# Another order of the attention's parts on all engines, and the strided probabilities normalised on GpSimd

## The chip, the core and the metric

The kernel runs on one core of a Trainium2 chip. The metric is the device time of one execution, in microseconds (us). The core has five engines that run at the same time, each through its own list of instructions in order: TensorE (PE; PEld is its weight load), VectorE (DVE), ScalarE (ACT), GpSimd (POOL) and SyncE (SP), which here only issues the DMA transfers. The transfers of SyncE's queue are carried by 16 DMA engines. Semaphores make an engine wait for another one.

## What is computed

Three stages follow each other: masked attention over 4 batches of 8 heads (576 positions, 64 channels), a soft mixture of 8 experts with 4 slots each, and a two-layer network with a squared ReLU. Half of the heads see a local window of 32 positions, the other half every 32nd position.

```python
scores = scale * np.matmul(q, k.transpose(0, 1, 3, 2))
mask_local = (rel >= 0) & (rel < stride)                       # heads 0 to 3
mask_strided = (rel >= 0) & (pos[None, :] % stride == pos[:, None] % stride)   # heads 4 to 7
attn = softmax(where(mask, scores, -1e9)); x = attn @ v        # x as (2304, 512)

logits = x @ phi
d = softmax(logits, over tokens); slot_input = d.T @ x         # 32 slots of 512
slot_out[e] = relu(slot_input[e] @ w1[e]) @ w2[e]              # 8 experts
y = softmax(logits, over slots) @ slot_out
out = relu(y @ w_in) ** 2 @ w_out
```

The expert weights are 33.5 MB in 64 pieces of 512 KB (`w1_slot`, `w2_slot`, issued at L120), q, k and v together some 14 MB. `w_in` and `w_out` come as 64-bit numbers and are narrowed on chip.

## The kernel before

Attention works on 16 units, each two heads of one batch. Even units are local, odd ones strided. A unit passes through these parts: `ld` (q and k loads; L379 and L390 for local, L385 and L390 for strided units; the L390 loads are small), `lv` (values: L399 local, L403 strided), `Tq` and `Tk` (transposes of q and k on TensorE, L501 and L503 or L506), `q` (ScalarE scales the transposed q out of PSUM, L525) and `k` (two copies on ScalarE, L488), `S` (scores, L550 to L574), `s` (maximum and subtraction on VectorE, L588 and L589 or L595 and L599), `e` (exponential on ScalarE, L610), `n` (strided units alone: sum, reciprocal and multiply, L617 to L620), `PT` (transposes of the probabilities, L629 or L634), `p` (their eviction: ScalarE for local units; for strided ones L648 on ScalarE and L650 on VectorE), `A` (times the values, L665 or L673), `a` (eviction, with the division for local units, L685 to L687), `X` and `x` (transposes of the output, L709 or L706, and eviction). For local units GpSimd copies the values once more, shifted by a block (`vs`, L410, two copies). After each four units `L` forms the logits (L728, L734), and `R1` to `R3` (L746 to L811) update the running softmax over tokens.

Two lists of words, `PIPE`, set the order. The program walks through the units u; at an even u it goes through the first list, at an odd u through the second, and `A-1` means part A of unit u-1. Each engine executes its own share of these parts in the order of the words (a pin ties each instruction of a computing engine behind the one before it). The DMA queue isn't pinned: a scheduler sorts its transfers when the program is built, and SyncE then issues them strictly in that order, so a transfer that waits for a buffer holds up those behind it. `ft` fetches weights: 1 or 2 pieces per unit in the first half of attention, 4 per pair in the second (`PACE`), into a ring of 27 buffers; buffers of attention are added to them as its last units finish. `cv` narrows one piece of `w_in` (L218 on ScalarE, L223 to L227 on VectorE). `F1` is a filler matmul on the mask (L153) that keeps TensorE at work; `DRAIN` sets more of them ahead of the last units' parts, and `KEEP` those in the end part of attention (`st_end`, L824).

All parts share PSUM as four pairs of banks. `pair` hands them out in turn, skipping the held ones; a part that gets a pair waits until its last user has been evicted. Which user that is follows from the order of the words.

After attention the experts' layers run pair by pair (L1030, L1060), freeing weight buffers as they go, and from about 183 us the last network (L1190, L1229) until the end.

The change touches `KEEP`, `DRAIN`, `PIPE` and `ON_ACT`. `ON_ACT` says for some evictions whether ScalarE does them: `pS` for the two halves of `p` of strided units, `n` for the engine of the multiply in `n` (0: VectorE; 2: GpSimd, but for the last unit).

## Time and profile before

| | |
|---|---|
| time, median of 3 runs (lowest to highest) | 418.67 us (415.93 to 420.39) |
| profiled execution | 419.13 us; the trace spans 417.2 us of it |
| busy in the span: PE, PEld, DVE, ACT, POOL | 387.8, 303.0, 238.5, 233.7, 86.7 us |
| chain that ended last | PE 64%, DMA 20%, DVE 5%, POOL 5% |
| mean granted TensorE clock | 0.979 of full speed |
| attention, expert layers, last network | to 147.6, to about 183, to 417 us |

The busy times say little on their own, since the stages have different limits. The rows further down are read by place: which stretch, what its engines do there, and who waits for whom. "PEclk" in them is the granted clock of TensorE as a share of 2.4 GHz, the DMA share the mean busy share of the 16 DMA engines (it goes over 1 where packets overlap).

### The profile page before, as it was taken

The numbers are of one execution on the slowest core, as the hardware profiler recorded it, in microseconds if no ns is written. First come the engines' busy times: TensorE is split into PE (matmuls) and PEld (weight loads), VectorE is DVE, ScalarE is ACT, GpSimd is POOL, SyncE is SP. The second block draws the span as 40 slices with busy tenths as digits, with TensorE's granted clock in tenths as the row PEclk, the third lists the DMA queues.
The fourth block names the chain that finished last, engine by engine and source line by source line (L and its number), as shares of the span: only waits on it lengthen the run. The fifth ranks groups of instructions, "written<-read, shape, count | busy, mean of one in ns | idle before, by whom it ended". The sixth has DMA issues, their size and how long they took to land.

```text
span 417.2 us, 9176 instructions
## 1 busy us (share of the span) xinstructions
PE 387.8 (93%) x3652; PEld 303.0 (73%) x3653; DVE 238.5 (57%) x452; ACT 233.7 (56%) x475; POOL 86.7 (21%) x121
## 2 busy tenths in 40 slices
PE   6898698989788899999999999999999999999996
PEld 3777486778666645467788887888887888878884
DVE  6456447766365461138856564867657766745434
ACT  3365536655543430039778686666666676666760
POOL 6302211102112020035610252111424103420000
PEclk9899779999899999999999999999999999999999
DMA  6897988998999999996212131221000000004033
GB/s 154 224 278 238 192 219 247 269 305 222 247 375 270 391 361 418 418 418 280 86 66 101 51 102 57 95 101 50 2 0 0 2 1 2 0 1 152 36 117 151
DMA packets 52202, 69.87 MB, mean 167 GB/s; under 512 B 31744, under 2 KB 37120, under 8 KB 52160
## 3 DMA queue, kind: packets, MB, share of 16 engines
q1 hardware_dynamic: 52160, 69.29, 51.9%
q8 instruction: 29, 0.48, 0.5%
q14 instruction: 13, 0.11, 0.1%
HBM read 64.55 MB, written 4.72 MB: 166 GB/s over the span
## 4 chain that ended last, share of the span: by engine, by line
PE 64%; DMA 20%; DVE 5%; POOL 5%; ACT 2%; issue 2%; SPq 2%; POOLq 0%; DVEq 0%; ACTq 0%
PE banks L1229 43%; DMA space<-in_v_dram 10%; DMA w<-in_moe_w_dram 7%; PE banks L1190 4%; DMA space<-in_k_dram 3%; PE banks L1030 2%; POOL space L410 2%; PE banks L665 2%; PE banks L1120 2%; PE banks L501 1%; POOL w L1105 1%; PE banks L554 1%; POOL w L1104 1%; PE banks L709 1%; PE banks L728 1%
## 5 line engine op out<-in xcount | busy, mean ns | idle before, releaser
L1229 PE MATMUL banks<-w 128*128 128x512 f32 x864 | 218.5, 395 | 1.6 <-POOL w L1105 1.2
L1229 PEld LDWEIGHTS banks<-w 128*128 128x128 f32 x864 | 159.5, 188 | 37.1 <-POOL w L1105 2.9
L1206 DVE TENSOR_TENSOR w<-r,w 128x384 fp32r<-128x384 f32 (+1 forms) x97 | 57.4, 594 | 73.0 <-ACT w L1205 72.9
L1197 ACT ACTIVATE r<-banks 128x384 f32<-128x384 f32 (+1 forms) x96 | 47.0, 490 | 53.1 <-PE banks L1190 46.2
L1203 ACT ACTIVATE r<-r 128x384 f32<-128x384 f32 (+1 forms) x96 | 50.3, 524 | 3.0
L1205 ACT CAST w<-r 128x384 fp32r<-128x384 f32 (+1 forms) x97 | 49.5, 510 | 4.1 <-DVE r L1202 0.6
L488 ACT COPY space<-banks 64x576 f32<-64x576 f32 (+2 forms) x64 | 34.7, 542 | 12.9 <-PE banks L153 10.3
L410 POOL COPY space<-space 32x1088 f32<-32x1088 f32 x16 | 17.7, 1107 | 103.0 <-DMA space<-in_v_dram 75.1
L220 POOL TENSOR_SCALAR nm<-w 128x512 f32<-128x512 f32 x28 | 24.0, 859 | 63.0 <-DMA w<-in_moe_w_out_dram 32.3
L1244 DVE TENSOR_TENSOR part<-banks,part 128x512 f32<-128x512 f32 (+1 forms) x55 | 34.9, 673 | 2.4 <-PE banks L1229 2.3
L1190 PE MATMUL banks<-cT,A 128*128 128x384 f32 x96 | 32.0, 335 | 0.0
L1104 POOL CAST w<-wf 128x512 fp32r<-128x512 f32 x16 | 11.8, 741 | 94.8 <-PE banks L1229 37.2
L501 PE MATMUL banks<-ident,space 128*128 128x128 f32 x128 | 22.8, 305 | 4.1 <-DVE space L589 2.4
L224 DVE SCALAR_TENSOR_TENSOR nm<-w,nm 128x512 uint32<-128x512 uint32 x32 | 22.3, 696 | 1.1
L501 PEld LDWEIGHTS banks<-ident,space 128*128 128x128 f32 x128 | 15.9, 161 | 8.1 <-DVE space L589 3.1
L1105 POOL TENSOR_TENSOR w<-wf,w 128x512 fp32r<-128x512 f32 x16 | 21.5, 1341 | 1.4
L223 DVE TENSOR_SCALAR nm<-nm 128x512 uint32<-128x512 uint32 x32 | 14.6, 457 | 12.3 <-POOL nm L220 9.2
L665 PE MATMUL banks<-space 128*32 128x130 f32 x288 | 13.7, 295 | 7.9 <-POOL space L410 4.8
L1190 PEld LDWEIGHTS banks<-cT,A 128*128 128x128 f32 x96 | 18.0, 188 | 3.9 <-ACT r L1197 0.2
L610 ACT ACTIVATE space<-space 128x640 f32<-128x640 f32 (+1 forms) x16 | 9.4, 590 | 17.4 <-DVE space L589 14.4
L488 DVE COPY space<-banks 128x576 f32<-128x576 f32 (+1 forms) x16 | 9.7, 607 | 15.9 <-ACT space L488 12.8
L665 PEld LDWEIGHTS banks<-space 128*32 128x32 f32 x288 | 9.7, 117 | 10.5 <-POOL space L410 6.4
(186 smaller groups left out, 446.2 us busy)
## 6 DMA issues: line engine op xcount, KB each, us to landing
w<-in_moe_w_dram SPq DMA_DIRECT2D x48, 512.0 KB
w<-in_moe_w_in_dram SPq DMA_DIRECT2D x16, 512.0 KB
space<-in_moe_w_dram SPq DMA_DIRECT2D x16, 512.0 KB
w<-in_moe_w_out_dram SPq DMA_DIRECT2D x16, 512.0 KB
space<-in_v_dram SPq DMA_DIRECT2D x32, 144.0 KB
out_dram<-part SPq DMA_DIRECT2D x17, 256.0 KB
space<-in_k_dram SPq DMA_DIRECT2D x16, 128.0 KB
space<-in_q_dram SPq DMA_DIRECT2D x16, 128.0 KB
```

Of the source, the lines that this page charges most:

```text
L410: nc.gpsimd.tensor_copy(vL[64 * h:64 * h + 32, 1:18, h, 0:D], vL[64 * h + 32:64 * h + 64, 0:17, h, 0:D])
L488: return (nc.scalar.copy if act else nc.vector.tensor_copy)(out=out, in_=in_)
L501: nc.tensor.transpose(out=pf[:, w * t:w * t + 128], in_=m[:, ts(t, 128)], identity=ident)
L665: nc.tensor.matmul(out=pv[c, n // 4] if n < 18 else pv[c, 4].rearrange("p (h e) -> p h e", h=2), lhsT=w, rhs=i, start=True, stop=True, til ...
L1105: nc.gpsimd.tensor_tensor(out=lo, in0=r, in1=hi.bitcast(F32), op=ALU.subtract)
L1190: nc.tensor.matmul(out=ps[:, 0:HB], lhsT=A4[c][:, ts(f % QF, 128)], rhs=cT4[:, c0:c0 + HB], start=True, stop=True)
L1197: nc.scalar.activation(out=r[:, cuts[0]], in_=ps[:, cuts[0]], func=AF.Relu)
L1203: nc.scalar.activation(out=r[:, cuts[0]], in_=r[:, cuts[0]], func=AF.Square)
L1205: nc.scalar.copy(out=gh[:, x], in_=r[:, x])
L1206: nc.vector.tensor_tensor(out=gl[:, x], in0=r[:, x], in1=gh[:, x].bitcast(F32), op=ALU.subtract)
L1229: nc.tensor.matmul(out=acc[t], lhsT=a[:, ts(t, 128)], rhs=wo[f][:, ts(w, 512)], start=(first and k == 0), stop=(last and k == 2),)
L1244: nc.vector.tensor_tensor(out=pt[:, cs], in0=acc[t][:, cs], in1=pt[:, cs], op=ALU.add)
```

## The change

The two lists of `PIPE` are rewritten; the strided multiply of `n` goes to GpSimd in seven of eight units; both halves of the strided `p` are done by VectorE; a few filler counts change. The table itself:

```diff
-KEEP = (4, 0, 0, 5, 0)
-DRAIN = dict(S0=0, PT1=0, A1=3, X1=4, PT0=4, A0=0)
+KEEP = (4, 0, 0, 8, 0)
+DRAIN = dict(S0=0, PT1=0, A1=3, X1=4, PT0=1, A0=1)
 PIPE = (
-    "PT-1 p-1 S+0 vs+0 x-3 ft Tq+1 s+0 R2 Tk+1 R3 X-2 e+0 cv q+1 ld+3 L-2 A-1 k+1 ld+4 R1 F1 F1 x-2 n+0 F1 F1 a-1".split(),
-    "lv+0 PT-1 cv p-1 S+0 s+0 Tq+1 q+1 e+0 Tk+1 A-1 n+0 k+1 lv+1 ft vs+0 L-2 X-2 a-1 R2 R1 R3".split(),
+    "PT-1 p-1 lv+0 S+0 x-3 Tk+1 ft s+0 Tq+1 L-2 R2 vs+0 R3 ld+3 q+1 X-2 e+0 R1 n+0 cv F1 ld+4 A-1 lv+1 x-2 k+1 F1 F1 F1 a-1".split(),
+    "PT-1 p-1 S+0 s+0 cv Tq+1 ft e+0 n+0 Tk+1 A-1 L-2 a-1 R2 k+1 vs+0 R1 X-2 q+1 R3".split(),
 )
-ON_ACT = dict(kL=(1, 1), kS=(1, 1), pL=1, pS=(1, 0), xL=0, xS=1, aS=(1, 1, 1, 0), q=1, n=0)
+ON_ACT = dict(kL=(1, 1), kS=(1, 1), pL=1, pS=(0, 0), xL=0, xS=1, aS=(1, 1, 1, 0), q=1, n=2)
```

Three places show what that does to the engines' lists. The first is the DMA queue in the pair of units 8 and 9: the local q and k of unit 12 (L379, L390), the strided values of unit 9 (L403) and weights (L120). Before:

```order
L379 DMA space<-in_q_dram 128x4x64 x2
L379 DMA space<-in_k_dram 128x4x64 x2
L390 DMA space<-in_k_dram 64x2x64
L390 DMA space<-in_q_dram 64x2x64
L403 DMA space<-in_v_dram 36x1024 x2
L120 DMA w<-in_moe_w_dram 128x1024 x4
```

The same place in the changed program:

```order
L379 DMA space<-in_k_dram 128x4x64 x2
L379 DMA space<-in_q_dram 128x4x64
L390 DMA space<-in_k_dram 64x2x64
L379 DMA space<-in_q_dram 128x4x64
L390 DMA space<-in_q_dram 64x2x64
L120 DMA w<-in_moe_w_dram 128x1024
L403 DMA space<-in_v_dram 36x1024 x2
L120 DMA w<-in_moe_w_dram 128x1024 x3
```

The keys now come before the queries, one small load moves ahead of the last large one, and one weight piece moves ahead of the strided values.

The second place is VectorE in the odd unit 7, where a piece of `w_in` is narrowed (L223 to L227). Before:

```order
L223 TENSOR_SCALAR nm<-nm 128x512
L224 SCALAR_TENSOR_TENSOR nm<-w,nm 128x512
L227 SCALAR_TENSOR_TENSOR wi<-w,nm 128x512
L595 TENSOR_REDUCE mx<-banks 128x2x4x2
L599 TENSOR_TENSOR space<-banks,mx 128x8x36
L617 TENSOR_REDUCE sm<-space 128x16
L618 TENSOR_SCALAR sm<-sm 128x16
L619 RECIPROCAL sm<-sm 128x16
L620 TENSOR_TENSOR space<-space,sm 128x8x36
```

The same place in the changed program:

```order
L595 TENSOR_REDUCE mx<-banks 128x2x4x2
L599 TENSOR_TENSOR space<-banks,mx 128x8x36
L223 TENSOR_SCALAR nm<-nm 128x512
L224 SCALAR_TENSOR_TENSOR nm<-w,nm 128x512
L227 SCALAR_TENSOR_TENSOR wi<-w,nm 128x512
L617 TENSOR_REDUCE sm<-space 128x16
L618 TENSOR_SCALAR sm<-sm 128x16
L619 RECIPROCAL sm<-sm 128x16
L685 TENSOR_SCALAR den<-banks 128x10
```

The maximum and the subtraction moved ahead of the narrowing, and the multiply (L620) is gone from VectorE. GpSimd has it instead, between the shifts of the local values (L410); its list in attention was fourteen L410 rows in a run, and begins now:

```order
L620 TENSOR_TENSOR space<-space,sm 128x8x36
L410 COPY space<-space 32x17x64 x2
L620 TENSOR_TENSOR space<-space,sm 128x8x36
L410 COPY space<-space 32x17x64 x2
L620 TENSOR_TENSOR space<-space,sm 128x8x36
```

So each multiply stands between the shift for the local unit before it and the shift for the one after it.

## Rows read from the trace of the kernel before

**Rows 1.** Stretches: us, busy (x count) of PE, PEld, DVE, ACT, POOL; PEclk, DMA share, GB/s
```profile
120.00:130.00 10.00, 8.63 (x154) 6.91 (x156) 4.69 (x9) 5.75 (x15) 0.00 (x0) 1.00 1.11 277
...
160.00:170.00 10.00, 10.00 (x156) 5.27 (x152) 1.04 (x2) 0.00 (x0) 0.00 (x0) 1.00 1.03 419
...
210.00:300.00 90.00, 89.67 (x449) 73.93 (x448) 57.01 (x100) 62.77 (x126) 22.63 (x24) 1.00 0.21 71
```
**Rows 2.** The chain that ended last: start us, us, what
```profile
169.47 9.91 DMA w<-in_moe_w_dram
```
**Rows 3.** Stretches in the later half of attention
```profile
82.00:86.00 4.00, 3.67 (x59) 2.98 (x61) 3.19 (x10) 2.54 (x5) 1.55 (x2) 1.00 0.55 165
96.00:100.00 4.00, 4.00 (x118) 3.64 (x118) 1.57 (x4) 3.03 (x7) 2.20 (x2) 1.00 0.49 115
```
**Rows 4.** Timeline of the DMA issues: start us, us, engine, line, transfer, count
```profile
75.93 1.83 SPq L379 DMA_DIRECT2D space<-in_q_dram  x2
...
80.84 0.62 SPq L390 DMA_DIRECT2D space<-in_k_dram  x1
...
82.22 0.92 SPq L403 DMA_DIRECT2D space<-in_v_dram  x2
83.19 2.65 SPq L120 DMA_DIRECT2D w<-in_moe_w_dram  x4
...
96.48 0.61 SPq L390 DMA_DIRECT2D space<-in_q_dram  x1
```
**Rows 5.** Timeline of TensorE, four of its waits: [idle before <- what ended it]
```profile
33.95 1.19 PE L665 MATMUL banks<-space 128*32 128x130 f32 x33 [1.33 <-POOL space L410]
...
49.85 2.16 PE L665 MATMUL banks<-space 128*32 128x130 f32 x33 [1.34 <-POOL space L410]
...
91.99 0.66 PE L501 MATMUL banks<-ident,space 128*128 128x128 f32 x4 [0.94 <-DVE space L589]
...
108.13 1.22 PE L673 MATMUL banks<-space 128*64 128x72 f32 x32 [2.25 <-DMA space<-in_v_dram]
```
**Rows 6.** Stretches at a lower granted clock
```profile
47.00:58.00 11.00, 8.76 (x88) 7.11 (x89) 2.63 (x8) 1.14 (x5) 2.36 (x2) 0.54 0.84 253
109.00:113.00 4.00, 4.00 (x89) 3.37 (x86) 0.92 (x2) 1.81 (x4) 0.00 (x0) 0.57 1.25 200
```
**Rows 7.** Timeline: multiply, transposes and eviction of the probabilities of unit 7
```profile
72.59 0.46 DVE L620 TENSOR_TENSOR space<-space,sm 128x288 f32<-128x288 f32 x1
...
73.20 0.63 PE L634 MATMUL banks<-ident,space 128*128 128x128 f32 x4 [1.34 <-DVE den L685]
...
73.92 0.89 ACT L648 ACTIVATE space<-banks,sub 64x288 f32<-64x288 f32 x2 [1.16 <-PE banks L634]
...
74.84 0.76 DVE L650 TENSOR_TENSOR space<-banks,sub 64x576 f32<-64x576 f32 x1 [0.60 <-ACT space L648]
```
**Rows 8.** Groups of the page: two-input subtractions on DVE and POOL (busy us, mean ns)
```profile
L1206 DVE TENSOR_TENSOR w<-r,w 128x384 fp32r<-128x384 f32 (+1 forms) x97 | 57.4, 594 | 73.0 <-ACT w L1205 72.9
...
L1105 POOL TENSOR_TENSOR w<-wf,w 128x512 fp32r<-128x512 f32 x16 | 21.5, 1341 | 1.4
```
**Rows 9.** Timeline: logits of the second batch, scores of unit 10, copy of the logits
```profile
85.92 1.08 PE L734 MATMUL banks<-space,phi 128*32 128x128 f32 x32
...
87.97 0.38 PE L550 MATMUL banks<-maskl,identb 128*128 128x512 bf16 x1
...
88.50 0.36 DVE L755 COPY space<-banks 128x192 f32<-128x192 f32 x1 [0.88 <-ACT space L752]
```
**Rows 10.** Timeline: ScalarE's copies and the scores of unit 9 that waited
```profile
79.10 3.19 ACT L488 COPY space<-banks 64x576 f32<-64x576 f32 x6
...
80.44 0.28 PE L566 MATMUL banks<-masks,identb 128*128 128x288 bf16 x1 [0.40 <-ACT space L488]
```
**Rows 11.** Timeline of TensorE: fillers at the end of attention
```profile
134.51 0.81 PE L153 MATMUL banks<-maskl,identb 128*128 128x384 bf16 x4
...
146.00 0.71 PE L824 MATMUL banks<-ident,identb 128*128 128x256 bf16 x5
```

## The prediction

> **What bounds the kernel now.** I read the stretches first, then the chain, then the waits of TensorE and the DMA queue. From 210 us on TensorE is busy 89.67 of 90 us [rows 1]; the change touches nothing there, so only the front, up to about 183 us, can move. The chain shows what ends the front: the expert weights, the last of which land at 169.47+9.91 = 179.4 us [rows 2]. Between 160 and 170 us the queue moves 419 GB/s, and from 120 to 130 us, in the middle of attention, the DMA share is already 1.11 [rows 1]. So late in the front a transfer comes earlier only if the engines of the DMA had idle time before. The reader should look for that idle time: the share is 0.55 in 82 to 86 us and 0.49 in 96 to 100 us [rows 3], 1.8 and 2.0 us of empty queue. Earlier gaps exist too, but there the queue waits for TensorE: the local query load of 75.93 us [rows 4] is issued when the query transposes of the next unit have read the buffer. Up to about 82 us TensorE's pace counts, after it the queue's. In that first part TensorE loses most to the local values: 1.33 us before 33.95 and 1.34 us before 49.85 us, behind the shift on GpSimd [rows 5], and then to the clock: 47 to 58 us run at a mean of 0.54 of full speed [rows 6], close to the level of 1.2 GHz, after TensorE had stood still.
>
> **The change, part by part.** *DMA queue.* Nothing is added or dropped. In each pair of units one small key load (0.62 us to issue, 80.84 us) goes ahead of the last query load, and one weight load goes ahead of the strided values, whose two issues take 0.92 us [rows 4]. At 82 us the first weights were issued at 83.19, behind the small loads and the values [rows 4]; they would now stand right after the last small load: 0.92 us sooner for the values, 0.62 us because one small load less is left behind the last large one. Together 1.5 of the gap's 1.8 us. At 96.48 us the weights already stand before the values, so only the 0.62 us are left. I count 2.1 us. Bounds: 0, if the small loads that moved ahead delay the large one by as much; 3.8 us, both gaps. The gaps before 82 us I count at nothing, since the next load there waits for TensorE; had they counted in the same way, three times 1.5 us would come off.
>
> *Normalisation on GpSimd.* Seven of eight multiplies leave VectorE, at 0.46 us each [rows 7]. The trace has none on GpSimd. The nearest rows are the subtractions, 1341 ns for 512 elements there and 594 ns for 384 on VectorE [rows 8]; per element that is a ratio of 1.7, so 0.46 becomes 0.78, say 0.80 us. Bounds: 0.46, and 1.34 as if size did not count. It lies before the strided transposes, which already waited 1.34 us for this chain at 73.20 [rows 7]. So each costs up to 0.34 us on the path where nothing hides it. In units 5, 9 and 13 the logit matmuls do (L734 alone takes 1.08 us [rows 9]); in 7 the conversion of a weight, which moves from before the maximum to behind the exponential's start, gives about as much back. I take +0.2 us for unit 3 and -0.1 for unit 7; unit 11 falls into the queue's part. The Trainium skill, GPSIMD Engine Reference, 3.1 Elementwise, measures 1.96 times VectorE's time for a two-input add. By that the multiply would be 0.90 us, and the sum 0.1 us longer.
>
> *Both halves of the strided eviction on VectorE.* ScalarE's two pieces (0.89 us) and then VectorE's one (0.76 us) were in series, 73.92 to 75.60 [rows 7]; now two of 0.76 are. That is 0.13 us less until the next maximum, and 0.89 us less ScalarE work per pair, not on the path: ScalarE's exponential waits for VectorE.
>
> *Key copies last.* In an even unit the query scaling now runs before the exponential, and the next probability transpose takes the PSUM pair that the key copy frees. Before, only the scores, one step later, waited for the keys: 80.44, 0.40 us behind ScalarE's copies from 79.10 [rows 10]. The transposes of a local unit's probabilities (about 0.6 us, an estimate: the four of a strided unit take 0.63 at 73.20 [rows 7]) would stand behind this wait instead of in front of it. So 0 to 0.6 us per unit; I take the middle, 0.3, since no row decides it, for units 2, 4 and 8: +0.9 us. In units 6 and 10 the state matmuls cover it, 12 lies in the queue's part.
>
> *Softmax state.* The scores of units 6, 10 and 14 now take the pair that the logits held. At 87.97 they began 0.9 us before VectorE had copied the logits out (88.50+0.36) [rows 9]; now they wait that long. In return both transposes come before the state's own, and the 0.94 us that the key transposes lost at 91.99 to the maximum's pair [rows 5] go. Count: 0.
>
> *First local values.* For unit 2 they are issued ahead of two strided loads. That could take away the 1.33 us before 33.95 [rows 5]. But the values of unit 4 are issued when the queue gets to them, and TensorE would wait the longer for those, so I count it at nothing.
>
> *Drain.* Three fillers fewer before the last transposes (four took 0.81 us [rows 11], so about -0.6), the eviction's -0.13, three more in the end part (five took 0.71 us [rows 11], so +0.4), and one that hides in a wait: -0.3 us.
>
> *Sum.* -2.1 + 0.2 - 0.1 + 0.9 + 0 - 0.3 is -1.4 us. The profiled execution took 419.13 us, of which the trace spans 417.2; the change would make it 417.7. It stood 0.46 us above the median of the runs, so I predict 417.3 us: no change that can be told, since about 1% is what a measurement of this kernel can tell from none.
>
> **Rivals.** *The half clock goes (faster).* If the values of unit 4 land sooner, because the weights fill the queue one issue earlier, TensorE's idle time ahead of 49.85 shrinks and the slow stretch of 47 to 58 us with it. At full speed the 8.76 us of TensorE work there [rows 6] would take about half, 4.4 us less: 412.9. For it: the slow stretch follows a wait for a transfer that the change moves. Against it: TensorE comes to that wait about a microsecond earlier, too, and stands longer.
>
> *The strided values come late (slower).* They now queue behind one weight load more (in unit 6 two), 0.524 MB at 419 GB/s, so 1.25 us. The strided output already waited 2.25 us for them at 108.13 [rows 5], and right after it the clock stood at 0.57 for 4 us [rows 6]. The wait would be 3.5 us there, which the next wait for local values partly swallows. It decides the sign if the same wait opens in two more pairs: each 2.5 us of wait and about 1.7 us of slow clock, some 6 us on top of the forecast: about 423.3. Against it: in the units up to 8 the trace shows no such wait.
>
> *The lock (a little slower).* VectorE's conversions read two SBUF operands, and GpSimd's multiply reads SBUF beside VectorE's work. Were each of seven multiplies held up by one such operation of about 0.7 us, 4.9 us would come on top: 422.2. The order speaks against it: the conversion comes before the sum on VectorE, on which the multiply waits. The Trainium skill, SBUF — State Buffer, Who interferes with whom, says that these two shut each other out for the whole instruction; no row here shows it.
>
> *The order does not matter.* The same bytes pass, the gap only moves behind another load, and TensorE pays its +0.7 us (the sum without the queue's -2.1) or more: 419 to 421.
>
> **How the numbers follow.** Forecast (415 to 419) 0.33, order without effect 0.22, half clock goes 0.23, late values 0.17, lock 0.05. Faster by over 1% (below 414.5) is the third case and a little of the first, 0.25; slower (above 422.9) is most of the fourth and part of the fifth, 0.20; the rest 0.55. The likeliest cases alone span 414.5 to 421. The range of 80% takes in most of both outer cases: 411 to 423.5.
>
> **What would show it.** Right: DMA share in 82 to 100 us without a slice near 0.5, the last weights landing about 1 to 2 us before 179.4, GpSimd's multiply at 0.7 to 0.9 us, and even units whose probability transposes wait for ScalarE. Wrong: a clock at full speed from 47 to 58 us, or the strided output waiting for values in more than three units, or the multiply over 1.1 us. The prediction fails altogether if attention's end moves by more than 4 us from 147.6 without the weights' end following, or if the part after 190 us takes another time.

## The result, and the profile after

| | before | changed |
|---|---|---|
| median (20 executions each, on the same chip) | 419.04 us (415.93 to 422.14) | 416.49 us (410.4 to 421.27) |
| mean, with its standard error | 418.99 +- 0.37 us | 416.18 +- 0.57 us |
| ratio, 95% interval | | 0.989 (0.9857 to 0.9923) |

The ratio leaves out executions that lie over 1.5% above the fastest of their kernel; one changed execution of 410.4 us is so far below the others that 9 ordinary ones fall out with that rule, so I also use means over all executions, and by them the gain is 2.8 us, or 0.7%. I predicted 417.3 us, with 411 to 423.5 as the range, and no change that can be told. The time is 0.8 us below the number (1.1 by the means), but the gain is twice the 1.4 us that my sum gave. Between 0.7% and 1.1% it stands at the edge of what a measurement tells.

The profiled execution of the changed kernel took 418.53 us, 2.3 us more than the mean, and its trace spans 416.8 us against 417.2 before. So the two traces can't show the gain as a difference of their lengths. They show what happens at each place. First the stretches (us, busy and count of PE, PEld, DVE, ACT, POOL; granted clock, DMA share, GB/s) of the changed kernel:

```profile
47.00:58.00 11.00, 9.08 (x102) 7.28 (x104) 4.14 (x12) 3.48 (x9) 2.86 (x3) 0.69 0.86 254
82.00:86.00 4.00, 2.92 (x50) 2.38 (x48) 2.25 (x7) 1.61 (x3) 2.37 (x3) 1.00 0.76 220
96.00:100.00 4.00, 4.00 (x119) 3.59 (x119) 1.56 (x4) 2.12 (x5) 2.20 (x2) 1.00 0.57 128
109.00:113.00 4.00, 2.46 (x35) 2.34 (x36) 0.00 (x0) 0.00 (x0) 0.00 (x0) 0.53 1.18 199
160.00:170.00 10.00, 10.00 (x156) 5.26 (x152) 1.28 (x2) 0.00 (x0) 0.00 (x0) 1.00 1.03 418
```

Against [rows 3] the gap at 82 us is smaller (share 0.76 for 0.55), the one at 96 us a little (0.57 for 0.49). Against [rows 6] the clock of 47 to 58 us stands at 0.69 instead of 0.54, and at 109 us it is as low as before. In a second profile of the changed kernel, `after_again`, TensorE runs at full clock from 47 to 58 us:

```profile
47.00:58.00 11.00, 9.85 (x158) 8.17 (x156) 6.01 (x14) 3.70 (x11) 2.54 (x3) 1.00 0.97 274
```

The reader should also look at the last line of the first table beside [rows 1]: from 160 to 170 us TensorE is busy for 10.00 of 10.00 us, in both kernels. That number, which I had in front of me, decides more than the DMA share beside it, as the experiments show.

Next, what TensorE waited for up to 150 us in the changed kernel (line, what released it: total us, times, longest):

```profile
PE banks L673 <- DMA space<-in_v_dram: 3.9, 2, 3.7
PE banks L665 <- POOL space L410: 3.7, 3, 1.4
PE banks L634 <- POOL space L620: 2.2, 2, 1.3
PE banks L629 <- ACT space L488: 2.0, 3, 1.0
PE banks L665 <- DMA space<-in_v_dram: 1.9, 2, 1.4
...
PE banks L550 <- DVE s_run L756: 1.6, 2, 0.8
```

All the waits that the prediction named for the new order are there: strided transposes behind GpSimd's multiply, local transposes behind the key copies, scores behind the logits' copy, strided output behind its values. The longest is the last, in unit 11:

```profile
106.47 0.33 PE L153 MATMUL banks<-maskl,identb 128*128 128x384 bf16 x1
110.54 2.19 PE L673 MATMUL banks<-space 128*64 128x72 f32 x32 [3.74 <-DMA space<-in_v_dram]
```

It was 2.25 us before [rows 5]. What became of the queue around 82 us (SyncE's issues: start us, us):

```profile
80.59 0.62 SPq L390 DMA_DIRECT2D space<-in_k_dram  x1
81.26 0.59 SPq L379 DMA_DIRECT2D space<-in_q_dram  x1
81.90 0.62 SPq L390 DMA_DIRECT2D space<-in_q_dram  x1
82.56 0.59 SPq L120 DMA_DIRECT2D w<-in_moe_w_dram  x1
83.26 1.57 SPq L403 DMA_DIRECT2D space<-in_v_dram  x2
84.87 1.30 SPq L120 DMA_DIRECT2D w<-in_moe_w_dram  x3
```

The first weight piece goes out 0.66 us after the last small load begins (81.90 to 82.56), where [rows 4] had the two strided values in between. And the strided unit 7, whose counterpart is [rows 7]:

```profile
70.83 0.25 DVE L619 RECIPROCAL sm<-sm 128x16 f32<-128x16 f32 x1
71.25 0.67 POOL L620 TENSOR_TENSOR space<-space,sm 128x288 f32<-128x288 f32 x1 [7.97 <-DVE den L685]
71.39 0.82 DVE L687 TENSOR_TENSOR xNb<-banks,den 128x640 f32<-128x640 f32 x1
71.98 0.66 PE L634 MATMUL banks<-ident,space 128*128 128x128 f32 x4 [1.32 <-POOL space L620]
72.74 1.52 DVE L650 TENSOR_TENSOR space<-banks,sub 64x576 f32<-64x576 f32 x2 [0.53 <-PE banks L634]
```

The multiply takes 0.67 us on GpSimd, and the division of the local unit (L687) runs beside it on VectorE instead of behind it. The strided transposes wait 1.32 us for it here, where they waited 1.34 us for VectorE before [rows 7].

Last, the weight load on TensorE that waits for the last expert weights, in the kernel before and in the changed one:

```profile
179.43 1.43 PEld L1060 LDWEIGHTS banks<-w,hT 128*32 128x32 f32 x26 [0.73 <-DMA w<-in_moe_w_dram]
```

```profile
179.23 1.43 PEld L1060 LDWEIGHTS banks<-w,hT 128*32 128x32 f32 x26 [0.29 <-DMA w<-in_moe_w_dram]
```

The weights come 0.2 us earlier here, not the 1 to 2 us that I had named as a sign of being right.

### The profile page after: what moved, and what is told of

It reads as the page before. It is cut to its first block, busy times and chain, and to the rows that moved or that the text cites. A ratio compares the mean times of both kernels' runs of the same rounds, so it can differ in the third digit from the quotient of the medians.

```text
span 416.8 us, 9152 instructions
## 1 busy us (share of the span) xinstructions
PE 387.3 (93%) x3654; PEld 302.3 (73%) x3654; DVE 242.6 (58%) x453; ACT 226.7 (54%) x459; POOL 90.8 (22%) x128
## 4 chain that ended last, share of the span: by engine, by line
PE 73%; DMA 9%; DVE 5%; POOL 4%; ACT 3%; SPq 3%; issue 2%; POOLq 0%; DVEq 0%; ACTq 0%
PE banks L1229 43%; DMA space<-in_v_dram 6%; PE banks L1060 4%; PE banks L1190 4%; PE banks L1030 3%; PE banks L501 2%; DMA w<-in_moe_w_dram 2%; PE banks L554 2%; PE banks L1120 2%; PE banks L665 1%; PE banks L673 1%; POOL w L1105 1%; PE banks L728 1%; PE banks L734 1%; POOL space L410 1%
## 5 line engine op out<-in xcount | busy, mean ns | idle before, releaser
L1229 PE MATMUL banks<-w 128*128 128x512 f32 x864 | 218.3, 394 | 1.6 <-POOL w L1105 1.2
L1229 PEld LDWEIGHTS banks<-w 128*128 128x128 f32 x864 | 159.3, 188 | 37.2 <-POOL w L1105 2.9
L488 ACT COPY space<-banks 64x576 f32<-64x576 f32 (+2 forms) x64 | 34.8, 543 | 19.5 <-PE banks L153 12.2
L410 POOL COPY space<-space 32x1088 f32<-32x1088 f32 x16 | 17.5, 1096 | 80.9 <-DMA space<-in_v_dram 57.6
L501 PE MATMUL banks<-ident,space 128*128 128x128 f32 x128 | 21.9, 297 | 1.6 <-DMA space<-in_q_dram 1.6
L224 DVE SCALAR_TENSOR_TENSOR nm<-w,nm 128x512 uint32<-128x512 uint32 x32 | 22.3, 696 | 1.1
L223 DVE TENSOR_SCALAR nm<-nm 128x512 uint32<-128x512 uint32 x32 | 14.6, 457 | 12.5 <-POOL nm L220 8.7
L525 ACT ACTIVATE space<-banks 128x576 f32<-128x576 f32 x16 | 10.4, 651 | 20.1 <-PE banks L506 15.9
L488 DVE COPY space<-banks 128x576 f32<-128x576 f32 (+1 forms) x16 | 9.7, 608 | 17.3 <-ACT space L488 13.5
L501 PEld LDWEIGHTS banks<-ident,space 128*128 128x128 f32 x128 | 15.7, 159 | 4.7 <-POOL w L437 2.5
```

Source lines behind the costliest of these rows:

```text
L488: return (nc.scalar.copy if act else nc.vector.tensor_copy)(out=out, in_=in_)
L501: nc.tensor.transpose(out=pf[:, w * t:w * t + 128], in_=m[:, ts(t, 128)], identity=ident)
L1229: nc.tensor.matmul(out=acc[t], lhsT=a[:, ts(t, 128)], rhs=wo[f][:, ts(w, 512)], start=(first and k == 0), stop=(last and k == 2),)
```

## The experiments

Each kernel ran 12 times, beside 32 to 35 runs of the kernel before on the same chip. The means over all executions, with the standard error of each (one execution of `values_first` and three of the kernel before, of 440 to 934 us, are left out):

| kernel | mean, us | ratio to before, 95% interval |
|---|---|---|
| before, all runs beside the experiments (114) | 418.93 +- 0.20 | |
| `before_again` | 418.24 +- 0.40 | 0.9997 (0.9956 to 1.0038) |
| changed kernel, all runs with those of the result (32) | 416.09 +- 0.42 | |
| `after_again` (the changed kernel) | 415.94 +- 0.59 | 0.9962 (0.9916 to 1.0008) |
| `lists_only` | 418.31 +- 0.46 | 0.9995 (0.9957 to 1.0033) |
| `engines_only` | 418.41 +- 0.56 | 0.9994 (0.9954 to 1.0033) |
| `old_fillers` | 415.44 +- 0.51 | 0.9954 (0.9916 to 0.9991) |
| `mul_on_vector` | 417.35 +- 0.36 | 0.9968 (0.9937 to 0.9998) |
| `keys_early` | 416.69 +- 0.35 | 0.9949 (0.9920 to 0.9978) |
| `fill_waits` | 418.32 +- 0.66 | 0.9975 (0.9938 to 1.0012) |
| `values_first` | 417.38 +- 0.70 | 0.9954 (0.9916 to 0.9992) |
| `half_back_on_scalar` | 416.11 +- 0.66 | 0.9918 (0.9879 to 0.9957) |
| `even_old` | 417.55 +- 0.64 | 0.9949 (0.9909 to 0.9988) |
| `odd_old` | 415.83 +- 0.57 | 0.9926 (0.9889 to 0.9963) |

How sure is a difference? The kernel before, run again under another name, came out 0.8 us below its other 102 runs (the 114 contain both), 1.7 standard errors. So a difference of 0.6 us between two rows is nothing, one of 1.4 us is likely but not sure, and only one of 2 us and more is plain. The changed kernel is meant by its 32 runs below, 416.09 us. The runs from `old_fillers` to `fill_waits` and those from `values_first` to `odd_old` were made on two other chips, where the changed kernel itself did not run; the kernel before took 418.8 and 419.0 us there, against 419.3 us beside `after_again`. The profiles are single executions, which differ by 2 us and more from one to the next; they are used for places, not for totals.

**Repeats, and each half alone.** `before_again` and `after_again` are the two kernels. `lists_only` is the kernel before with the new `PIPE` and nothing else of the change; `engines_only` is the kernel before with the new `ON_ACT` alone:

```diff
-ON_ACT = dict(kL=(1, 1), kS=(1, 1), pL=1, pS=(1, 0), xL=0, xS=1, aS=(1, 1, 1, 0), q=1, n=0)
+ON_ACT = dict(kL=(1, 1), kS=(1, 1), pL=1, pS=(0, 0), xL=0, xS=1, aS=(1, 1, 1, 0), q=1, n=2)
```

> The kernel before, unchanged, so that each of its executions comes with its granted clock. My theory (the queue's gaps): the time at the lower clock level, (1 - mean clock) x 2 x span, is about the 17.7 us of the profiled execution in both kernels, and the changed kernel is faster by its order. Rival (the clock): the executions of before have more time at the lower level, 16 us or more in the mean against 11.5 us in the 20 of the changed kernel, and at equal time at the lower level the two kernels differ by less than 1 us. In the changed kernel each us at the lower level goes with 0.36 us of span, from 410.2 us without any; the rival expects the same line here.

> The changed kernel, unchanged, for a second profile and more executions beside those of before on the same chip. Both theories expect 2 to 4 us less than before in the mean (2.8 us over the 20 executions so far). The gap theory expects a DMA share of 0.70 or more in 82 to 86 us again (before: 0.55); the clock theory expects less time at the lower level than before, whatever the gaps.

> The kernel before with the two new lists alone: multiply on VectorE, half of the strided eviction on ScalarE, old filler counts. Gap theory: the order of the queue comes from the lists, so most of the gain is here, 2 to 3 us less than before, and at most 0.5 us more when the engines change too. Rival (engines): the gain comes from relieving ScalarE, so the lists alone bring less than 1 us or cost something, because the late key copies then wait behind the 0.89 us of eviction that ScalarE keeps.

> The kernel before with the new engine choices alone: seven multiplies on GpSimd (0.67 us each in the changed kernel's trace), both halves of the strided eviction on VectorE; old lists and fillers. Gap theory: within 1 us of before, since the old lists keep the queue's order and TensorE waits 0.2 us longer per multiply. Rival (engines): 2 us or more faster, since each pair of units loses 0.89 us of ScalarE.

The gain repeats: 415.94 us against 418.93. Neither half alone brings it; each is worth 0.5 to 0.6 us against the kernel before, which is within the noise. So either the two need each other or something else in the change, the fillers, does it.

**The filler counts back.**

```diff
-KEEP = (4, 0, 0, 8, 0)
-DRAIN = dict(S0=0, PT1=0, A1=3, X1=4, PT0=1, A0=1)
+KEEP = (4, 0, 0, 5, 0)
+DRAIN = dict(S0=0, PT1=0, A1=3, X1=4, PT0=4, A0=0)
```

> The changed kernel with the filler counts of before (KEEP and DRAIN): both lists and both engine moves together, nothing else. In the runs so far the lists alone and the engine moves alone each took 0.6 to 0.7 us off the kernel before (about 418.4), while the whole change took about 3 us off (416.1). Theory (the two parts work only together): 416.1, within 1 us of the changed kernel. Rival (the fillers ahead of the last units and in the end part do it): 417.5 to 418.4, as either part alone. In the profile the first keeps attention's end and the end of the expert layers where the changed kernel has them; the second has attention end 1 to 2 us later than there.

415.44 us: the fillers are not it. With both lists and both engine moves, and the old fillers, the gain is all there.

This completes a square: the kernel before, the lists alone, the engine moves alone, and both, all with the old fillers. With the new lists the engine moves bring 2.9 +- 0.7 us (418.31 to 415.44), with the old ones 0.5 +- 0.6. With the engine moves the lists bring 3.0 +- 0.8 us (418.41 to 415.44), without them 0.6 +- 0.5. So each half is needed: without either of them 2 to 3 us of the gain are gone, which is plain. Both together bring 2.4 +- 0.9 us more than the two apart (1.8 +- 1.0 if only runs of one chip are taken, with the changed kernel for both), so it is likely that each is worth more beside the other. Through which wait, no profile shows.

**The multiply back on VectorE.**

```diff
-ON_ACT = dict(kL=(1, 1), kS=(1, 1), pL=1, pS=(0, 0), xL=0, xS=1, aS=(1, 1, 1, 0), q=1, n=2)
+ON_ACT = dict(kL=(1, 1), kS=(1, 1), pL=1, pS=(0, 0), xL=0, xS=1, aS=(1, 1, 1, 0), q=1, n=0)
```

> The changed kernel with the strided multiply back on VectorE in all units. The prediction gave the move to GpSimd +0.2 us in unit 3 and -0.1 in unit 7, with 0.80 us for each multiply. Measured on GpSimd it is 0.67 us against 0.46 on VectorE, and the strided transposes wait for it twice (0.93 and 1.32 us). Theory (the move is nearly neutral): the waits of the strided transposes stay, now behind VectorE, shorter by 0.2 us each or longer by what VectorE has queued ahead; time within 0.6 us of the changed kernel. Rival (VectorE, rid of the multiplies, is what makes the two parts work together): 417.5 to 418.4, with VectorE's narrowing and evictions holding up the transposes in three or more units.

417.35 us, 1.3 us above the changed kernel (2.3 standard errors of the difference). I had expected no more than 0.6. Unit 7 of this kernel's profile, the same rows as above:

```profile
70.72 0.25 DVE L619 RECIPROCAL sm<-sm 128x16 f32<-128x16 f32 x1
71.01 0.46 DVE L620 TENSOR_TENSOR space<-space,sm 128x288 f32<-128x288 f32 x1
71.61 0.63 PE L634 MATMUL banks<-ident,space 128*128 128x128 f32 x4 [0.98 <-DVE den L685]
71.83 0.82 DVE L687 TENSOR_TENSOR xNb<-banks,den 128x640 f32<-128x640 f32 x1
72.57 1.51 DVE L650 TENSOR_TENSOR space<-banks,sub 64x576 f32<-64x576 f32 x2
```

From the end of the reciprocal to the start of the transposes it is 0.64 us here (70.97 to 71.61) and 0.90 in the changed kernel (71.08 to 71.98). From there to the evicted probabilities it is 3.11 us (70.97 to 74.08) against 3.18 (71.08 to 74.26): what the multiply loses on GpSimd, the division that runs beside it gives back. So this unit's chain says that the two places of the multiply cost the same, and the time says that they may not.

In another unit the chain does get longer. In unit 5, GpSimd's shift holds VectorE up:

```profile
46.44 2.25 POOL L410 COPY space<-space 32x1088 f32<-32x1088 f32 x2 [12.73 <-DMA space<-in_v_dram]
46.53 1.03 DVE L618 TENSOR_SCALAR sm<-sm 128x16 f32<-128x16 f32 x1
47.89 1.12 DVE L620 TENSOR_TENSOR space<-space,sm 128x288 f32<-128x288 f32 x1
```

L618 takes 0.17 us and the multiply 0.46 where no shift runs beside them; here they are 0.86 and 0.66 us longer. On GpSimd the multiply can't meet the shift in this way: it stands behind it in the same list. But TensorE comes to these probabilities only at 55.94 us, so in this execution the hold-up costs nothing that can be seen. The edit also let the scheduler change two places of the DMA queue at 30 to 36 us, where two strided values now go ahead of a weight piece and a small key load ahead of a query load. Where the 1.3 us come from, if they are real, stays open.

**The key copies early again.** In the even list:

```diff
-... q+1 X-2 e+0 R1 n+0 cv F1 ld+4 A-1 lv+1 x-2 k+1 F1 F1 F1 a-1
+... q+1 k+1 X-2 e+0 R1 n+0 cv F1 ld+4 A-1 lv+1 x-2 F1 F1 F1 a-1
```

> The changed kernel with the key copies of the even list moved from its end to just behind the query scaling, ahead of the exponential. This tests the prediction's largest cost, +0.9 us for the key copies as the last part. Theory: the waits of the local units' probability transposes for ScalarE's key copies (2.0 us in three units in the changed kernel's profile) vanish, and the time falls by 0.5 to 1 us, to about 415.3. Rival (the wait only moves): the exponential starts about 1 us later in every even unit, so the same transposes wait for the exponential instead, or the output transposes and scores that follow do; time equal or up to 1.5 us longer.

416.69 us, 0.6 us above the changed kernel, with an error of 0.55: nothing of the expected gain. TensorE's waits up to 148 us:

```profile
PE banks L501 <- DVE space L488: 5.4, 3, 2.4
PE banks L629 <- ACT space L610: 3.5, 5, 1.6
PE banks L665 <- POOL space L410: 2.6, 3, 1.2
```

The wait of L629 for the key copies is gone from the list, and five of L629 for the exponential have come, 3.5 us in place of 2.0. The rival was right in this execution: the wait only moves, since both are ScalarE's work ahead of the same transposes. The edit isn't clean, though. With it the scheduler issues the local values of unit 2 at 26.85 us, behind the strided loads, instead of at 23.07, and the key transposes (L501) wait 5.4 us for key copies (L488), which they did not do in the changed kernel.

**Fillers in the waits for values.** 8, 8 and 16 filler matmuls ahead of the output of units 2, 4 and 11:

```diff
-DRAIN = dict(S0=0, PT1=0, A1=3, X1=4, PT0=1, A0=1)
+DRAIN = dict(S0=0, PT1=0, A1=3, X1=4, PT0=1, A0=1, A13=8, A11=8, A4=16)
```

> The changed kernel with filler matmuls (8, 8 and 16, about 0.2 us each) ahead of the values of units 2, 4 and 11, where TensorE stands still for 2.6, 1.9 and 3.7 us and the granted clock falls to half afterwards in the changed kernel's profile. Theory (the idle time before the values costs a second time through the clock, as in the prediction's first rival): the time at the lower clock falls from about 12 us per execution to below 6 us, and the time by 1 to 2 us, to 414 to 415. Rival (the clock is not what the change gained by, since the next wait for a transfer takes up what a slow stretch loses): less time at the lower clock, but 416 or, where fillers run longer than the wait, up to 417.5.

418.32 us, 2.2 us above the changed kernel: nearly all the gain is lost, which neither expectation had. At the place itself the fillers did what they should, and the wait stands somewhere else:

```profile
75.62 2.19 PE L673 MATMUL banks<-space 128*64 128x72 f32 x32 [3.58 <-DMA space<-in_v_dram]
...
105.10 2.93 PE L153 MATMUL banks<-maskl,identb 128*128 128x384 bf16 x17
107.96 1.22 PE L673 MATMUL banks<-space 128*64 128x72 f32 x32
```

In unit 11 seventeen fillers ran while the values came, and the output followed at once and at full clock (granted clock 1.00 from 105 to 113 us), in 1.22 us instead of the 2.19 in the changed kernel. But in unit 7 TensorE now stood still for 3.58 us for its strided values, and its output took 2.19 us there. This is one execution; in it the late transfer was met four units earlier.

The time at the lower of the clock's two levels (twice the span times what the mean granted clock lacks to 1, as a mean over all executions) fell from 11.6 and 12.2 us in the two sets of the changed kernel to 9.1 us. It is 16 to 18 us in the kernel before, 14.1 in `lists_only`, 16.2 in `engines_only`, and 12.2 in `mul_on_vector`, which has as little of it as the changed kernel and is slower. Each of these means has an error of about 1 to 2 us. So the clock's lower level goes along with the order, but it can't be the whole gain: two kernels with as little or less of it are slower. A straight line through the executions of each kernel gives 0.02 to 0.36 us of span for each microsecond of it, and 0.14 +- 0.02 through all 265 executions, each taken against the mean of its own set. By that the 4 to 6 us less of it would go with 0.6 to 0.8 us of the gain of 2.8 (an estimate). The fillers themselves took 0.56, 0.56 and 2.9 us; how much of that fell outside a wait in the other executions isn't shown.

**The values ahead of the weights.** The changed kernel with every strided load of units 3 to 13 ahead of the weight piece; TensorE's, VectorE's, ScalarE's and GpSimd's lists are untouched. Two strided query loads fall behind other loads with it:

```diff
-                nc.sync.dma_start(
-                    out=vS[64 * h:64 * h + 36], in_=src.rearrange("(p c) d -> p c d", c=16)
-                )
+                late = nc.sync.dma_start(
+                    out=vS[64 * h:64 * h + 36], in_=src.rearrange("(p c) d -> p c d", c=16))
+                pace[0] = late if u < 13 else pace[0]
```

> The changed kernel in which each strided load of values (units 3 to 13) is issued ahead of the weight piece that the new order puts before it; nothing on the computing engines differs. It tests the prediction's largest term, the queue's gap of -2.1 us, of which 1.5 us came from the weights standing right behind the last small load, and the rival of late strided values. Theory of the prediction: the gap at about 82 us opens again (DMA share below 0.6 there) and the time rises by about 1.5 us, to about 417.5. Rival (late values): the strided output of unit 11, which waited 3.7 us for its values in the changed kernel's profile, waits under 2.3 us, and the time falls by 1 to 2 us, to 414 to 415. Third reading (the order of the queue doesn't matter): within 0.6 us of the changed kernel's 416.

417.38 us, 1.3 us above the changed kernel: the size that the prediction gave (1.5 us), with an error of 0.8, so likely at best. In its profile the place of the gap stands 3.3 us earlier than in the kernel before, so the window has to move with it. The issues there, and the stretch from 0.5 us behind the start of the last small load (L390) on, which is 82 to 86 us in the kernel before:

```profile
78.20 0.62 SPq L390 DMA_DIRECT2D space<-in_q_dram  x1
78.91 0.92 SPq L403 DMA_DIRECT2D space<-in_v_dram  x2
79.88 1.77 SPq L120 DMA_DIRECT2D w<-in_moe_w_dram  x4
```

```profile
78.70:82.70 4.00, 2.73 (x39) 2.13 (x39) 0.21 (x2) 0.00 (x0) 1.86 (x3) 0.64 0.79 208
```

The same stretch in the changed kernel:

```profile
82.39:86.39 4.00, 2.92 (x58) 2.38 (x62) 2.53 (x6) 1.36 (x3) 1.98 (x3) 1.00 0.82 230
```

The weights stand 1.68 us behind the small load, as in the kernel before (0.66 in the changed one), and the share is 0.79 all the same: the gap did not open again to below 0.6. One stretch of one execution says little, however. At this place the share is 0.51 to 0.71 in the four profiles with the queue of before, and 0.78 to 0.90 in seven of the nine with the new one, but 0.61 in `fill_waits` and 0.45 in `lists_only`.

And the waits up to 148 us:

```profile
PE banks L665 <- DMA space<-in_v_dram: 4.9, 3, 1.9
PE banks L665 <- POOL space L410: 4.7, 4, 1.4
PE banks L629 <- ACT space L488: 2.6, 4, 1.0
```

The strided output no longer waits for its values, as the rival said. But the local output waits so much longer, for its values and for the shift that follows them, that the sum is the same: 4.9 + 4.7 = 9.6 us here, and 3.9 + 3.7 + 1.9 = 9.5 us in the changed kernel. In this execution, then, the transfer that is put first seems to take its time from the next one. It isn't a rule: the three waits add up to 8.1 us in `after_again`, and to 10.0 and 9.5 us in the two profiles of the kernel before.

**One half of the strided eviction back on ScalarE.**

```diff
-ON_ACT = dict(kL=(1, 1), kS=(1, 1), pL=1, pS=(0, 0), xL=0, xS=1, aS=(1, 1, 1, 0), q=1, n=2)
+ON_ACT = dict(kL=(1, 1), kS=(1, 1), pL=1, pS=(1, 0), xL=0, xS=1, aS=(1, 1, 1, 0), q=1, n=2)
```

> The changed kernel with the strided eviction as before: ScalarE does one half, VectorE the other. The prediction gave this part -0.13 us, and nothing else to it. Putting the multiply back on VectorE cost 1.3 us though the profile showed no longer chain in any unit; this run completes the square. Theory (it is small, and in the profile's chain from reciprocal to evicted probabilities it is within 0.3 us): 416, within 0.6 us of the changed kernel. Rival (both engine moves are needed with the new lists): about 417.3, as with the multiply put back.

416.11 us: with the multiply on GpSimd this part is worth nothing that can be measured, as expected. That `mul_on_vector` showed no longer chain in any unit is wrong: unit 5's was longer.

**One list of before, the other new.** `even_old` has the even list of before (and with it, row by row, the DMA queue of before); `odd_old` has the odd list of before, and the queue of the changed kernel. The loads of values, which before stood in the odd list, stay with the queue they belong to (in `even_old` two words, `lv+0` and `lv+1`, go back into the odd list):

```diff
 even_old:
-    "PT-1 p-1 lv+0 S+0 x-3 Tk+1 ft s+0 Tq+1 L-2 R2 vs+0 R3 ld+3 q+1 X-2 e+0 R1 n+0 cv F1 ld+4 A-1 lv+1 x-2 k+1 F1 F1 F1 a-1".split(),
+    "PT-1 p-1 S+0 vs+0 x-3 ft Tq+1 s+0 R2 Tk+1 R3 X-2 e+0 cv q+1 ld+3 L-2 A-1 k+1 ld+4 R1 F1 F1 x-2 n+0 F1 F1 a-1".split(),
 odd_old:
-    "PT-1 p-1 S+0 s+0 cv Tq+1 ft e+0 n+0 Tk+1 A-1 L-2 a-1 R2 k+1 vs+0 R1 X-2 q+1 R3".split(),
+    "PT-1 cv p-1 S+0 s+0 Tq+1 q+1 e+0 Tk+1 A-1 n+0 k+1 ft vs+0 L-2 X-2 a-1 R2 R1 R3".split(),
```

> The changed kernel with the even list of before; the odd list is the new one, with the loads of values back at the two places that they had in it before. So the whole DMA queue stands in the order of before, and the key copies of the even units stand ahead of the fillers as before; the odd list and both engine moves are new. Theory (the even list carries the gain, by the queue and by the end of the half-clock waits): 418 to 419. Rival (the odd list with the engine moves carries it: the narrowing moved into the shadow of the exponential): 416, within 0.7 us of the changed kernel.

> The changed kernel with the odd list of before (without its loads of values, which the new even list issues); the DMA queue stands in the new order throughout, and both engine moves are new. Theory (the even list and its queue carry the gain): 416, within 0.7 us of the changed kernel. Rival (the odd list carries it): 417.5 to 418.5, with the local probabilities' or outputs' steps waiting for VectorE's narrowing, which stands ahead of the maximum again. Both this and the run with the old even list near 418 would mean that only the two lists together give it.

The old odd list changes nothing (415.83 us). The old even list costs 1.5 us (417.55 us, 1.9 standard errors), about what another order of the queue cost in `values_first`; both are likely, not sure.

What the profile of `even_old` shows is worth more than its mean. By chance this execution is the shortest of all that were profiled, 411.0 us in the trace. The first and last start of the expert layers' first matmuls (L1030) and of the last network's (L1229), in the kernel before:

```profile
L1030 PE MATMUL banks<-w,sT x104: 592/592/617, 147.6 to 170.3; 128*32 128x512 f32 x104
L1229 PE MATMUL banks<-w x864: 386/393/502, 186.7 to 412.9; 128*128 128x512 f32 x173
```

In the changed kernel:

```profile
L1030 PE MATMUL banks<-w,sT x104: 592/592/617, 147.8 to 170.6; 128*32 128x512 f32 x104
L1229 PE MATMUL banks<-w x864: 387/393/502, 186.6 to 412.5; 128*128 128x512 f32 x173
```

In `even_old`:

```profile
L1030 PE MATMUL banks<-w,sT x104: 592/592/617, 142.3 to 165.0; 128*32 128x512 f32 x104
L1229 PE MATMUL banks<-w x864: 387/393/500, 180.7 to 406.8; 128*128 128x512 f32 x173
```

Attention ends 5.3 us earlier than before, and the last network starts 6.0 us earlier: 39.1, 38.8 and 38.4 us lie between the two first starts, and 226 us between the first and the last of L1229. Over all 14 profiles the last L1060 matmul ends 33.0 to 34.4 us after the first L1030 starts. TensorE's waits for weights in that stretch, in the kernel before and in `fill_waits`, where they are longest:

```profile
PE banks L1060 <- DMA w<-in_moe_w_dram: 0.2, 1, 0.2
```

```profile
PE banks L1060 <- DMA w<-in_moe_w_dram: 0.9, 1, 0.9
```

The changed kernel and `even_old` have none. So the weights do not set when the front ends. TensorE goes through the expert layers in 33.0 us from wherever attention ends, and late weights add 0 to 1.4 us to that: 0.7 us in the kernel before, 0.3 in the changed one, 1.4 in `fill_waits`, `lists_only` and `odd_old`. That is small beside the 5.8 us by which attention's end differs, but not beside the differences between the means above. That the weights come along because attention holds the queue back too is argued, not shown.

## Why the prediction was right or wrong, point by point

**What bounds the kernel: wrong.** I read the last weights' landing off the chain [rows 2] and made it the bound, and from that I held that up to 82 us TensorE's pace counts and after it the queue's. The chain follows one string of releases, and at a near tie it goes through the DMA: in the kernel before the wait it hangs on is 0.2 us long. In the changed kernel the same chain has 73% on TensorE and 9% on DMA (64% and 20% before), while the expert layers take nearly as long (33.3 and 33.7 us). TensorE's 10.00 us in [rows 1] said so. What can move by more is attention's end, through TensorE's waits and the queue as far as it feeds them.

**The queue's gap, -2.1 us: perhaps the right size, and not by this way.** Putting the values first again costs 1.3 us (+- 0.8) where I had 1.5 for the 82 us part. But at its place the gap is hardly wider in `values_first` (share 0.79) than in the changed kernel (0.82), and there, where the share rose from 0.55, so that about 1 us of idle queue is gone, the last weights land only 0.2 us earlier. So idle time ahead of the last weights is not what the order of the queue is worth. The even list with its queue is likely worth 1.5 us; how it reaches attention's end the profiles don't show, since a single execution can't show 1.5 us when they differ by several. This stays open.

**The multiply on GpSimd, +0.1 us: the duration was near, the term has the wrong sign, if anything.** Seven multiplies took 0.671 to 0.675 us, against my 0.80 and within 0.7 to 0.9 but for 0.03. The ratio to VectorE's 0.457 is 1.47. The estimate from the subtraction's rows (1.7) was closer than the 1.96 that the Trainium skill, GPSIMD Engine Reference, 3.1 Elementwise, gives for an add of 2048 elements; the measurement decides. The waits that it set stood in the units 1 and 7 (1.32 us at 71.98; 2.2 us together; VectorE set 2.1 us there before), not in unit 3, where I had put one. Putting it back cost 1.3 +- 0.55 us with the new lists. The two engine moves together brought 2.9 +- 0.7 us with the new lists and 0.5 +- 0.6 with the old ones; my sum had no term for parts that help each other. I took only what the multiply itself adds to the unit's chain, and left out what VectorE does beside it (L687), which makes up for it. That gets to zero; the rest is unexplained.

**Key copies last, +0.9 us: the waits came, the cost did not.** L629 waited 0.36, 0.95 and 0.68 us in three units, 2.0 us in all against 0.9, in the units 2, 4 and 8 as expected. Taking the waits away made the kernel no faster (0.6 +- 0.55 us slower, with unit 2's values later in the queue as well), and 3.5 us of the same transposes behind the exponential came in. The step that failed is counting a wait on an engine's queue as a cost without asking what stands there if the queue is turned round.

**Softmax state, 0: about right.** Two waits of 0.78 us behind the logits' copy and the addition after it (0.9 expected in three units) replaced three of up to 0.94 us [rows 5], 1.6 us for 2.4.

**Strided eviction, -0.13, and the drain, -0.3: too small to be seen**, and nothing was seen.

**First local values, 0: about right in sum, the other way round.** They were issued at 23.07 instead of 24.25 us but took 8.96 us to land, at 32.03, and TensorE waited 2.6 us for them and their shift, where it had waited 1.3. In unit 4, where I had expected the longer wait, it fell from 3.7 to 1.9 us.

**The rivals.** The values came late in unit 11 by just what I had worked out (3.74 us, 3.5 expected), in no second pair. In `after_again` there is a second one, 1.40 us in unit 7 beside 3.15 in unit 11, so that rival came near its sign. Its price was too low by its own terms: two pairs of 2.5 + 1.7 us are 8.4 us, not 6.

The half clock went in part, 4 to 6 us of it per execution. In `after_again` its stretch of 47 to 58 us is at full speed, which I had named as a sign of being wrong. By the estimate above it is worth 0.6 to 0.8 us of the gain, far less than the 4.4 us that I gave it.

The lock did not touch GpSimd's multiply, which takes the same 0.67 us seven times. L687 keeps its 0.82 us beside it, but it reads PSUM (`banks`), and none of the conversions that I had in mind ran beside a multiply in this profile. Between VectorE and GpSimd's shift, which I had not priced, the hold-up is there in the changed kernel too:

```profile
81.51 2.25 POOL L410 COPY space<-space 32x1088 f32<-32x1088 f32 x2 [9.58 <-DMA space<-in_v_dram]
83.10 0.69 DVE L618 TENSOR_SCALAR sm<-sm 128x16 f32<-128x16 f32 x1
```

L618, which takes 0.17 us elsewhere, ends when the shift does, at 83.8 us. The order did matter: with the new engines the lists are worth 3.0 +- 0.8 us, of which the old odd list takes nothing away.

**The number.** That 417.3 was within 0.8 us is in part luck. The sum gave a gain of 1.4 us, and 2.6 (medians) to 2.8 us (means) came; the median of before rose from 418.67 to 419.04 us with more runs, a cost of 1.0 us (multiply and keys) did not come, about 1 us of gain from the multiply was not foreseen, and the queue, credited with 2.1 us where about 1.3 was measured, hid a part of both. The parts' measured prices (1.3 for the queue, 1.3 for the multiply, 0.6 for the keys, nothing for the rest) add up to 3.2 us beside 2.8 us for the whole. If the halves help each other, prices taken one at a time need not add up, and with errors of 0.6 to 0.8 each this proves no single one.

## What to carry to other kernels

Before a transfer at the end of the chain is called the bound, look up how long the engine really waited for it: here 0.2 us, in a stretch where that engine was busy all the time. Where several transfers share a queue, putting one first can move the wait to the next, so sum the waits for all of them. When two runs are compared at a place, let the window follow the place in the program: here it had moved by 3.3 us. Change the parts alone and together before they are priced, since here two halves that were worth 0.5 and 0.6 us alone brought 3.5 us together (+- about 0.5 each). And a list of waits from one execution ranks places; it doesn't price them when executions differ by more than the effect.

## What the runs showed of the hardware

- Executions of one and the same kernel differ by up to 11 us (410.4 to 421.27 for the changed kernel). In the 14 that were profiled the difference lies in attention, which ends between 142.3 and 148.1 us; from the first L1229 start to the end it is 230.3 to 231.0 us in all of them.
- The time at the lower clock level is 9 to 18 us per execution on average, depending on the order of work. At that level the same strided output took 2.19 us instead of 1.22, so a microsecond of it loses nearly half a microsecond; at the end it goes with only 0.14 +- 0.02 us, so the larger part is paid back. That it falls beside waits for transfers, which then are shorter, would explain it; no run tried that by itself.
- VectorE and GpSimd's shift (L410, a copy from SBUF to SBUF of 1.1 us) hold each other up. Beside it L618 took up to 1.08 us instead of 0.17 (changed kernel), L620 1.12 and 1.18 instead of 0.46 (`mul_on_vector`, `lists_only`), L227 1.55 instead of 0.69 (`keys_early`), and one shift took 1.60 us behind L224 (`after_again`).
- A local values' load that was issued 1.2 us earlier landed 0.5 us later (23.07 + 8.96 us against 31.53).
- A f32 multiply of 128x288 with a broadcast operand takes 0.457 us on VectorE, where no shift runs beside it, and 0.674 us on GpSimd.
